# Sparse attention ahead of two expert layers: values' products in runs of four, tails' transposes between the score products, the normaliser's operations one per iteration

## The chip, the core and the metric

One core of a Trainium2 chip runs the whole program. The metric is device time in microseconds (us); lower is better. Five engines work side by side, each in its own program order, and wait for each other by semaphores: TensorE (PE in the rows; its weight loads are PEld), VectorE (DVE), ScalarE (ACT), GpSimd (POOL) and SyncE (SP, which issues most DMAs). Matrix products end in PSUM, which has eight banks of 512 f32 columns on 128 partitions.

## The reference, cut to what matters

```python
def _attn_ref(q, k, v, tau):                     # 4 batches, 8 heads, 576 tokens, 64 columns
    scores = 1.0 / np.sqrt(64) * np.matmul(q, k.transpose(0, 1, 3, 2))
    thresh = np.max(scores, axis=-1, keepdims=True) - tau
    scores = np.where(scores >= thresh, scores, -1000000000.0)
    attn = np.exp(scores - np.max(scores, axis=-1, keepdims=True))
    attn = attn / (np.sum(attn, axis=-1, keepdims=True) + 1e-09)
    return np.matmul(attn, v)
```

The result, as 2304 rows of 512, goes through a layer of eight experts (each row goes to its best one: 512 to 1024, relu, back to 512, times its gate) and then through a dense layer (512 to 2048, x times sigmoid(1.702 x), back to 512).

## The kernel before, in words

**Units and iterations.** Attention works on 16 pairs of heads, four per batch. A pair is cut into nine *units*, w = 0 to 8. Units 0 to 7 are 128 queries (chunk c) of one head (h) each, with w = 2c + h; unit 8 holds the last 64 queries of both heads, and its score product takes eight matmuls instead of four. `run` goes through 144 units, two per *iteration*; 72 iterations make scores, a 73rd only finishes. Nine iterations are a *round*: two pairs. Place k is the iteration's number modulo 9; unit 8 stands first in place 4 and second in place 8.

**An iteration.** In the order in which they are written, which is the order on each engine:

- PE: `qk` of the first unit (score products into two of four PSUM banks `sc`), `trans` of the first unit of the iteration before (four transposes into a bank `tr`), then `qk` and `trans` of the second units, then work that is dealt out by tables: *items* of the values' products (`AV`), `trans_tails`, items of output rows (`ROW`). In the last batch other tables (`AVL`, `ROWL`) count, and items of the router are dealt between.
- DVE: `max` of both units (reads `sc`, line 250), `mask` of both (reads `sc` again, line 280).
- ACT: a copy of the first transposes (`AT`, line 309), `exp` of both units, a copy of the second transposes, then copies of what the dealt work left in PSUM.

`qk` of a unit writes the two banks that `mask` of the unit two before it read, so the first `qk` of an iteration waits for the first `mask` of the iteration before it.

**Values' products.** For each half of a pair's 576 queries (288 columns) `av_items` makes a *tail item* (one product with all 128 columns of `Vt`, line 349) and four *main items* (each one product for each head, 64 columns of the array wide, line 353), all added up in the one bank `av`; after the last, ACT copies it to `xT` (line 358). All ten items of a pair are queued when the pair's last unit has been transposed. On the chip each of these f32 products is two matmuls, so a row of a main item counts four and a tail item two.

**Tails.** Keys 512 to 575 of both heads are transposed by `trans_tails`: after units 3 and 8, behind the iteration's values' products, with one ACT copy of 256 columns each (line 334) and two more copies of 64 by 64 behind unit 8 (line 337).

**Normaliser and rows.** Behind the `mask` of the last unit of every second pair, four small DVE operations (lines 286 to 289) make `r`. A row item (`row_items`) is four matmuls on `xT` (line 383), an ACT copy `xr` (line 388), two POOL products with `r` (lines 391 and 396) and DMAs of `xrow` to `x_dram`; `xr` and `xrow` have two buffers each. When all five row items of the second half of a batch are out, the router of that batch is queued.

**Hand-over.** What is left of the values' and row items behind the 73rd iteration is drained by `tail`, partly between the first transposes (line 947) and products (line 975) of the first expert slot.

```python
            for i in range(2):
                if i < len(us):
                    self.qk(us[i])
                if i < len(ts):
                    copies += self.trans(ts[i])
            ...
            n = AVL[it - IT_LAST] if last else AV[it % 9]
            while n and avq:
                avq.pop(0)()
                n -= 1
            for u in ts:
                self.trans_tails(u)
```

Of the kernel before, what the change touches and what calls it, by code (L numbers as in the profile page):

```python
# [33 lines left out]
CO = (0, 3)  # L34
# [13 lines left out]
ROW = (1, 1, 0, 0, 0, 1, 0, 1, 1)  # L48

class Attention:  # L50
# [16 lines left out]
    def __init__(self, ctx, late_ctx, tc, kq, v, tau, w_gate, x_dram, router, ident, ps):  # L67
# [4 lines left out]
        self.ps_sc, self.ps_tr, self.ps_av = ps  # L72
        P = lambda name, bufs, **kw: ctx.enter_context(tc.tile_pool(name=name, bufs=bufs, **kw))
        Q = lambda name, bufs: late_ctx.enter_context(tc.tile_pool(name=name, bufs=bufs, side="right"))
# [27 lines left out]
        self.extra = []  # L102

# [122 lines left out]
    def qk(self, u):  # L226
        nc = self.nc
        p, w = divmod(u, UPP)
        d = self.st[p]
        sc = self.ps_sc.tile([128, 2, 512], F32, name="sc")  # L230
        d["sc", w] = sc
        if w < 8:
            c, h = divmod(w, 2)
            ops = [(d["qT"][:, h * 768 + c * 128:h * 768 + (c + 1) * 128], kk, h * 704) for kk in ("kA", "kB")]
        else:
            ops = [(d["qT"][:, 512 + h * 128:640 + h * 128], kk, h * 768) for h in range(2) for kk in ("kA", "kB")]
        for hf in range(2):
            for i, (l, kk, c0) in enumerate(ops):
                nc.tensor.matmul(  # L239
                    sc[:, hf, 0:288], l, d[kk][:, c0 + hf * 288:c0 + (hf + 1) * 288],  # L240
                    start=(i == 0), stop=(i == len(ops) - 1),
                )

    def max(self, u):
# [5 lines left out]
        nc.vector.tensor_scalar(  # L250
            e, d["sc", w][:, :, 0:288], self.taue[:, 0:1], 3.0e38, op0=ALU.add, op1=ALU.min, accum_out=thr)
# [6 lines left out]
    def mask(self, u):  # L258
# [17 lines left out]
        else:  # L276
# [3 lines left out]
        nc.vector.scalar_tensor_tensor(  # L280
            out=E.rearrange("p (a c) -> p a c", a=2), in0=d["sc", w][:, :, 0:288],
            scalar=d["thr", w][:, 0:1], in1=d["e", w], op0=ALU.is_le, op1=ALU.mult, accum_out=acc,
        )
        if hp % 2 and w == 8:
            h0 = 2 * hp - 2
            nc.vector.tensor_copy(rs[0:64, 4, h0:h0 + 4:2], rsT[0:64, hp - 1:hp + 1])
            nc.vector.tensor_copy(rs[0:64, 4, h0 + 1:h0 + 4:2], rsT[64:128, hp - 1:hp + 1])
            nc.vector.tensor_scalar_add(r[:, :, h0:h0 + 4], rs[:, :, h0:h0 + 4], 1e-9)
            nc.vector.reciprocal(r[:, :, h0:h0 + 4], r[:, :, h0:h0 + 4])


    def trans(self, u):
# [9 lines left out]
        copies = []  # L302
# [5 lines left out]
        if w < 8:  # L308
            copies.append(lambda: nc.scalar.copy(  # L309
                AT[:, h, :, c * 128:(c + 1) * 128], tp.rearrange("p (k c) -> p k c", k=4)))  # L310
        else:
            copies.append(lambda: nc.scalar.copy(
                AT[:, :, :, 512:576].rearrange("p h k c -> p k h c"),
                tp.rearrange("p (k h c) -> p k h c", k=4, h=2)))
        return copies

    def trans_tails(self, u):
# [3 lines left out]
        if w not in (3, 8):  # L321
            return
        d = self.st[p]
        ATt = d["ATt"]
        c0 = 0 if w == 3 else 2
        t2 = self.ps_tr.tile([128, 512], F32, name="tr")
        for i in range(2):
            nc.tensor.transpose(  # L328
                t2[:, i * 128:(i + 1) * 128],
                d["E", c0 + i].rearrange("p h s -> p (h s)")[:, 512:640], self.ident,  # L330
            )
        if w == 8:
            nc.tensor.transpose(t2[0:64, 256:384], d["E", 4][:, 512:576], self.ident)
        nc.scalar.copy(ATt[:, c0 * 128:(c0 + 2) * 128], t2[:, 0:256])
        if w == 8:
            for i in range(2):
                nc.scalar.copy(ATt[i * 64:(i + 1) * 64, 512:576], t2[0:64, 256 + i * 64:320 + i * 64])


    def av_items(self, p):  # L340
# [3 lines left out]
        xT = self.xT[b, hp] = self.xtp.tile([128, S], F32, name="xT")  # L344
        items = []
        for hf in range(2):
            def tail(hf=hf):
                d["av"] = self.ps_av.tile([128, 512], F32, name="av")
                nc.tensor.matmul(d["av"][:, 0:288], d["Vt"], d["ATt"][:, hf * 288:(hf + 1) * 288], start=True, stop=False, skip_group_check=True)  # L349

            def main(kc, hf=hf):
                for h in range(2):
                    nc.tensor.matmul(  # L353
                        d["av"][h * 64:(h + 1) * 64, 0:288], d["V"][:, h, kc, :],
                        d["AT"][:, h, kc, hf * 288:(hf + 1) * 288], start=False, stop=(kc == 3), skip_group_check=True,
                    )
                if kc == 3:
                    nc.scalar.copy(xT[:, hf * 288:(hf + 1) * 288], d["av"][:, 0:288])
                    if hf == 1:
                        del self.st[p]  # L360

            items.append(tail)
            items += [lambda kc=kc, m=main: m(kc) for kc in range(4)]
        return items
# [44 lines left out]
    def run(self):  # L409
# [12 lines left out]
        while done < NU:  # L422
# [4 lines left out]
            for p in starts:  # L427
# [4 lines left out]
                for n in range(1 if p == 0 else p + 2, min(p + 3, NPAIR)):  # L432
                    self.operands(n)
                    self.poolq += [lambda n=n, i=i: self.split(n, i, NPC) for i in range(NPC)]
            copies = []
            for i in range(2):
                if i < len(us):
                    self.qk(us[i])
                if i < len(ts):
                    copies += self.trans(ts[i])  # L440
# [1124 lines left out]
```

## Time and profile before

| what | value |
|---|---|
| time, median of 3 (lowest to highest) | 936.72 us (936.5 to 938.41) |
| profiled execution: its own time | 940.83 us |
| profiled execution: span of the trace | 939.1 us |
| mean granted clock of TensorE | 0.994 |
| PE, DVE, ACT, POOL busy | 900.9, 515.6, 454.2, 224.7 us |

A busy PE is not a PE at its peak: matmuls overlap in the rows. In a row of the trace in order of time stand the start (us from the span's start), the duration, engine, line, operation, names (output<-inputs), and in brackets the idle time before it and who ended it. Attention takes the first 305 us of the span.

### The profile page before, as it was taken

What the parts mean: (1) busy time and instruction counts of PE and PEld (TensorE: products, weight loads), DVE (VectorE), ACT (ScalarE), POOL (GpSimd) and SP (SyncE); (2) the same over time, 40 slices, a digit from 0 to 9 for tenths busy, and PEclk for the clock granted to TensorE, in tenths of its full rate; (3) what the DMA queues carried; (4) which work ended last, traced back from release to release, by engine and by line L of the source; (5) the groups of instructions that cost most, each with busy time, mean ns of one, the idle gap of its engine ahead of it and who ended that gap; (6) DMA issues with size and microseconds to landing.
All of it is one profiled execution on the core that took longest, in us unless ns stands there. A gap on an engine that the chain in (4) does not pass through costs nothing.

```text
span 939.1 us, 13971 instructions
## 1 busy us (share of the span) xinstructions
PE 900.9 (96%) x5015; PEld 735.8 (78%) x5015; DVE 515.6 (55%) x1129; ACT 454.2 (48%) x820; POOL 224.7 (24%) x299
## 2 busy tenths in 40 slices
PE   8899999999988999999999999999999999999994
PEld 7677777777766578878888988888888888888894
DVE  6788888888889357477777568821211111211110
ACT  6677777777766343445464545522222222222221
POOL 4746565665613220110440000010001000100100
PEclk9999999999999999999999999999999999999998
DMA  7755765656422633656665354410001000100100
GB/s 208 175 139 145 195 177 151 147 127 157 107 49 52 191 124 100 199 172 221 194 214 203 112 149 151 150 45 1 23 23 46 6 12 6 45 0 1 45 1 25
DMA packets 64523, 100.72 MB, mean 107 GB/s; under 512 B 10596, under 2 KB 35970, under 8 KB 64450
## 3 DMA queue, kind: packets, MB, share of 16 engines
q1 hardware_dynamic: 61138, 89.84, 33.1%
q0 software_dynamic: 3312, 9.94, 3.3%
q8 instruction: 42, 0.69, 0.3%
q14 instruction: 31, 0.25, 0.1%
HBM read 63.97 MB, written 17.11 MB: 86 GB/s over the span
## 4 chain that ended last, share of the span: by engine, by line
PE 77%; DVE 8%; issue 6%; DMA 3%; POOL 2%; ACT 2%; SPq 1%; POOLq 0%; ACTq 0%; DVEq 0%
PE tr L975 28%; PE sc L1000 19%; PE sc L1019 9%; PE sc L239 8%; PE av L353 5%; PE tr L307 4%; DVE e L250 3%; DVE E L280 2%; PE tr L383 1%; PE av L349 1%; ACT e L256 1%; PE tr L328 1%; DMA xg<-x_dram,igaA 1%; PE av L947 1%; SPq L176 1%
## 5 line engine op out<-in xcount | busy, mean ns | idle before, releaser
L1212 DVE TENSOR_TENSOR hl<-sg,hh 128x512 fp32r<-128x512 f32 (+1 forms) x80 | 51.0, 638 | 262.2 <-ACT hh L1210 262.2
L1209 ACT ACTIVATE sg<-tr 128x512 f32<-128x512 f32 (+1 forms) x80 | 44.3, 554 | 228.1 <-PE tr L975 228.1
L250 DVE TENSOR_SCALAR_CACHE_REDUCE e<-sc,taue 128x576 f32<-128x576 f32 x144 | 116.6, 813 | 33.5 <-PE sc L239 28.5
L256 ACT ACTIVATE e<-e,thr 128x576 f32<-128x576 f32 x144 | 111.3, 776 | 29.5 <-DVE e L250 28.8
L239 PE MATMUL sc<-kA,qT 128*128 128x288 f32 x320 | 103.0, 338 | 14.9 <-DVE E L280 11.0
L1000 PE MATMUL sc<-wo_h,hh 128*128 128x512 f32 x288 | 112.2, 390 | 0.0
L1000 PE MATMUL sc<-wo_l,hh 128*128 128x512 f32 x288 | 112.2, 390 | 0.0
L1000 PE MATMUL sc<-wo_h,hl 128*128 128x512 f32 x288 | 112.0, 389 | 0.0
L280 DVE SCALAR_TENSOR_TENSOR E<-sc,thr,e 128x576 f32<-128x576 f32 x128 | 103.6, 815 | 8.4 <-ACT e L256 4.4
L309 ACT COPY AT<-tr 128x512 f32<-128x512 f32 x128 | 74.0, 578 | 39.5 <-PE tr L307 39.4
L239 PE MATMUL sc<-kB,qT 128*128 128x288 f32 x320 | 90.0, 297 | 2.0 <-DMA kB<-kB 1.1
L239 PEld LDWEIGHTS sc<-kA,qT 128*128 128x128 f32 x320 | 60.7, 190 | 32.0 <-issue 20.0
L975 PE MATMUL tr<-xl,wi_h 128*128 128x512 f32 (+1 forms) x320 | 78.7, 368 | 0.0
L975 PE MATMUL tr<-xh,wi_l 128*128 128x512 f32 (+1 forms) x320 | 78.7, 368 | 0.0
L975 PE MATMUL tr<-xh,wi_h 128*128 128x512 f32 (+1 forms) x320 | 78.6, 368 | 0.0
L307 PE MATMUL tr<-ident,E 128*128 128x128 f32 x512 | 76.8, 272 | 0.0
L353 PE MATMUL av<-AT,V 128*64 128x288 f32 x512 | 76.7, 419 | 0.0
L975 PEld LDWEIGHTS tr<-xh,wi_h 128*128 128x128 f32 x320 | 57.6, 188 | 11.1
L975 PEld LDWEIGHTS tr<-xh,wi_l 128*128 128x128 f32 x320 | 56.9, 188 | 10.0
L975 PEld LDWEIGHTS tr<-xl,wi_h 128*128 128x128 f32 x320 | 56.9, 189 | 10.0
L239 PEld LDWEIGHTS sc<-kB,qT 128*128 128x128 f32 x320 | 61.0, 191 | 3.0 <-DVE kB L220 1.3
L1000 PEld LDWEIGHTS sc<-wo_h,hl 128*128 128x128 f32 x288 | 54.1, 188 | 11.4
(219 smaller groups left out, 1562.8 us busy)
## 6 DMA issues: line engine op xcount, KB each, us to landing
ra<-in_moe_w_dram SPq DMA_DIRECT2D x20, 512.0 KB, 3.6
rb<-in_moe_w_dram SPq DMA_DIRECT2D x20, 512.0 KB, 3.9
F<-in_kq_dram SPq DMA_DIRECT2D x15, 640.0 KB, 5.1
cv_raw<-in_moe_w_in_dram SPq DMA_DIRECT2D x16, 512.0 KB, 4.8
cv_raw<-in_moe_w_out_dram SPq DMA_DIRECT2D x16, 512.0 KB, 3.7
V<-in_vp_dram SPq DMA_DIRECT2D x16, 320.0 KB, 4.6
kA<-kA SPq DMA_DIRECT2D x15, 320.0 KB, 3.3
kB<-kB SPq DMA_DIRECT2D x15, 320.0 KB, 3.6
```

Of the source, the lines that this page charges most:

```text
L239: nc.tensor.matmul(sc[:, hf, 0:288], l, d[kk][:, c0 + hf * 288:c0 + (hf + 1) * 288], start=(i == 0), stop=(i == len(ops) - 1),)
L250: nc.vector.tensor_scalar(e, d["sc", w][:, :, 0:288], self.taue[:, 0:1], 3.0e38, op0=ALU.add, op1=ALU.min, accum_out=thr)
L256: self.nc.scalar.activation(d["e", w], d["e", w], ACTF.Exp, bias=d["thr", w][:, 0:1], scale=-1.0)
L280: nc.vector.scalar_tensor_tensor(out=E.rearrange("p (a c) -> p a c", a=2), in0=d["sc", w][:, :, 0:288], scalar=d["thr", w][:, 0:1], in1=d[ ...
L307: nc.tensor.transpose(tp[:, kc * 128:(kc + 1) * 128], E[:, k0 + kc * 128:k0 + (kc + 1) * 128], self.ident)
L309: copies.append(lambda: nc.scalar.copy(AT[:, h, :, c * 128:(c + 1) * 128], tp.rearrange("p (k c) -> p k c", k=4)))
L353: nc.tensor.matmul(d["av"][h * 64:(h + 1) * 64, 0:288], d["V"][:, h, kc, :], d["AT"][:, h, kc, hf * 288:(hf + 1) * 288], start=False, stop ...
L975: nc.tensor.matmul(hps[:, 0:T], w[:, kd, :], blk[x][:, kd, 0:T], start=(i == 0), stop=(i == 11))
L1000: nc.tensor.matmul(y, h[:, cs], w, start=(f == 0 and i == 0), stop=(f == blk["nf"] - 1 and i == 2))
L1019: nc.tensor.matmul(blk["y"][d], w[:, ds], h[:, 0:T], start=(f == 0 and i == 0), stop=(f == last and i == 2))
L1209: nc.scalar.activation(sg, hps, ACTF.Gelu_apprx_sigmoid)
L1212: return [upper, lambda: nc.vector.tensor_sub(hl, sg, hh.bitcast(F32))]
```

## The change

- **Values' products.** The tail item goes behind the four main items of its half instead of ahead of them. The tables give four main items to one iteration and the tail item to the next: `AV` is 4, 1, 4, 1, 0, 4, 1, 4, 1 by place. A half's items are queued by `trans_tails`, so the first half of a pair starts before its last units. `AV1`, which put one item between the two score products in place 6, is gone. Rows are queued by the last tail item, and one row item goes out per iteration at places 1, 3, 4, 6 and 8.
- **Tails.** `trans_tails` is called in places 4, 6, 8 and 1, between the first `trans` and the second `qk`; it transposes three chunks behind unit 5, and behind unit 8 the fourth chunk and the last queries, so that one ACT copy does where three did. There are six transposes per pair instead of five. ACT's copy of them stands ahead of both `exp`.
- **Normaliser.** The four DVE operations are put in a list, and one is taken per iteration, ahead of the two `mask`.
- **Score banks.** The four banks are one tile; which unit uses which two is as before. Accesses to different banks are declared independent by hand, and the score products no longer wait for PE's own earlier products.
- **Last batch.** `AVL` and `ROWL` follow the same scheme; the 73rd iteration takes a whole half.

```diff
-AV = (3, 2, 3, 2, 3, 3, 2, 2, 2)
+AV = (4, 1, 4, 1, 0, 4, 1, 4, 1)
+TURNS = ((0, 1), (2, 3))
+TAILS = {4: -3, 6: -4, 8: -2, 1: -3}
...
-AVL = (3, 2, 3, 3, 2, 3, 2, 3, 2, 3, 2, 3, 2, 3, 2, 3, 1, 3, 0, 3, 2, 3)
-ROWL = (0, 3, 2, 2, 2, 1, 2, 2, 2, 2, 2, 0, 2, 3, 2, 2, 1, 2, 2, 2, 2, 2)
-AV1 = (0, 0, 0, 0, 0, 0, 1, 0, 0)
+AVL = (4, 1, 4, 1, 0, 4, 1, 4, 1, 4, 1, 4, 1, 0, 4, 1, 4, 1, 5)
+ROWL = (0, 1, 0, 1, 1, 1, 1, 1, 1, 0, 0, 0, 0, 1, 1, 1, 1, 1, 1)
...
-ROW = (1, 1, 0, 0, 0, 1, 0, 1, 1)
+ROW = (0, 1, 0, 1, 1, 0, 1, 0, 1)
...
+            self.norm += [
+                lambda: nc.vector.tensor_copy(rs[0:64, 4, h0:h0 + 4:2], rsT[0:64, hp - 1:hp + 1]),
+                lambda: nc.vector.tensor_copy(rs[0:64, 4, h0 + 1:h0 + 4:2], rsT[64:128, hp - 1:hp + 1]),
+                lambda: nc.vector.tensor_scalar_add(r[:, :, h0:h0 + 4], rs[:, :, h0:h0 + 4], 1e-9),
+                lambda: nc.vector.reciprocal(r[:, :, h0:h0 + 4], r[:, :, h0:h0 + 4]),
+            ]
...
+        cs = range(3) if w == 5 else range(3, 4)
+        n = len(cs) * 128
         t2 = self.ps_tr.tile([128, 512], F32, name="tr")
+        if w == 8:
+            nc.tensor.transpose(t2[:, 64:192], d["E", 4][:, 448:576], self.ident)
+            nc.tensor.transpose(t2[0:64, 128:256], d["E", 4][:, 512:576], self.ident)
+            n += 64
...
+        self.avq += self.av_items(p, w // 8)
+        return lambda: nc.scalar.copy(ATt[:, cs[0] * 128:cs[0] * 128 + n], t2[:, 0:n])
...
+        def tail():
+            nc.tensor.matmul(d["av"][:, 0:288], d["Vt"], d["ATt"][:, cols], start=False, stop=True, skip_group_check=True)
+            nc.scalar.copy(xT[:, cols], d["av"][:, 0:288])
+            if hf == 1:
+                del self.st[p]
+                if p % 2:
+                    while self.norm:
+                        self.norm.pop(0)()
+                    self.rowq.extend(self.row_items(b, hp // 2))
+
+        return [lambda kc=kc: main(kc) for kc in range(4)] + [tail]
...
+                    copies.append(self.trans(ts[i]))
+                if i == 0 and it > 1 and k in TAILS:
+                    copies.append(self.trans_tails(2 * it + TAILS[k]))
             for i in range(2):
+                while i == 0 and len(copies) > 1:
+                    copies.pop(0)()
                 if i < len(us):
                     self.max(us[i])
                     self.exp(us[i])
...
+            for c in copies:
+                c()
             while rest:
                 rest.pop(0)()
+            if self.norm:
+                self.norm.pop(0)()
...
+        self.trans_tails(NU - 1)()
```

Three places in the program show what moves on PE. The first is the end of iteration 47 and the start of iteration 48 (place 2, then place 3), from the second unit's transposes (`tr<-ident,E`) through the dealt work to the next score products (`sc`). Before:

```order
L307 MATMUL tr<-ident,E 128x128 x3
L353 MATMUL av<-AT,V 64x288 x6
L328 MATMUL tr<-ident,E 128x128 [waits Activation_49]
L328 MATMUL tr<-ident,E 128x128
L239 MATMUL sc<-kA,qT_135 128x288 [waits DVE_49,PE_49]
```

After:

```order
L330 MATMUL tr<-ident,E 128x128 x3
L374 MATMUL av<-AT,V 64x288 [waits Activation_49]
L374 MATMUL av<-AT,V 64x288 x7
L244 MATMUL sc<-kA,qT_136 128x288 [waits DVE_49]
L244 MATMUL sc<-kB,qT_136 128x288
```

Three main items (six products) have become four (eight), the two tails' transposes are gone from here, and the score product waits for DVE alone. The second place is iteration 51 (place 6), from the first unit's transposes to the second unit's score products. Before:

```order
L307 MATMUL tr<-ident,E 128x128 [waits Activation_49]
L307 MATMUL tr<-ident,E 128x128 x3
L349 MATMUL av<-ATt,V 128x288 [waits DMAHW3_49,Activation_49]
L239 MATMUL sc<-kA,qT_136 128x288 [waits DVE_49]
L239 MATMUL sc<-kB,qT_136 128x288
```

After:

```order
L330 MATMUL tr<-ident,E 128x128 [waits Activation_49]
L330 MATMUL tr<-ident,E 128x128 x3
L348 MATMUL tr<-ident,ET 128x128 [waits Activation_49]
L349 MATMUL tr<-ident,ET 64x128
L352 MATMUL tr<-ident,E 128x128
L244 MATMUL sc<-kA,qT_137 128x288 [waits DVE_49]
```

Where one tail item stood ahead of the second score products, three tails' transposes stand now; places 1, 4 and 8, which had nothing there, have them too. The third place is the hand-over, from the last transposes of attention (`ET`) to the first products of the first expert slot (`xh`); `xg` are that slot's gathered rows, `G,xT` is a row item's product. Before:

```order
L353 MATMUL av<-AT,V 64x288 x6
L349 MATMUL av<-ATt,V 128x288
L353 MATMUL av<-AT,V 64x288 x2
L947 MATMUL tr<-ident,xg 128x128 x4
L353 MATMUL av<-AT,V 64x288 x4
L947 MATMUL tr<-ident,xg 128x128 x4
L353 MATMUL av<-AT,V 64x288 x2
L349 MATMUL av<-ATt,V 128x288
L947 MATMUL tr<-ident,xg 128x128 x4
L353 MATMUL av<-AT,V 64x288 x4
L947 MATMUL tr<-ident,xg 128x128 x4
L353 MATMUL av<-AT,V 64x288 x4
```

After:

```order
L374 MATMUL av<-AT,V 64x288 x8
L380 MATMUL av<-ATt,V 128x288
L968 MATMUL tr<-ident,xg 128x128 x4
L414 MATMUL tr<-G,xT 128x144 x4
L968 MATMUL tr<-ident,xg 128x128 x4
L414 MATMUL tr<-G,xT 128x144 x4
L968 MATMUL tr<-ident,xg 128x128 x4
L414 MATMUL tr<-G,xT 64x144 x2
L968 MATMUL tr<-ident,xg 128x128 x4
L996 MATMUL tr<-xh,ah 128x512 x4
```

Before, thirteen values' items stand behind the last transposes, mostly between those of `xg`, and all five row items follow the slot's first group of products; after, ten values' items stand ahead of `xg`, the five row items stand between its transposes, and nothing is left behind the first group.

## Rows read from the trace of the kernel before

**Rows 1.** The page: span and number of instructions.
```profile
span 939.1 us, 13971 instructions
```

**Rows 2.** Groups, us 83 to 226.11; count | busy us, mean ns | idle before, ended by.
```profile
L250 DVE TENSOR_SCALAR_CACHE_REDUCE e<-sc,taue 128x576 f32<-128x576 f32 x72 | 58.1, 813 | 15.3 <-PE sc L239 12.9
L239 PE MATMUL sc<-kA,qT 128*128 128x288 f32 x160 | 51.3, 338 | 4.1 <-DVE E L280 4.1
```

**Rows 3.** DVE in order of time, iterations 45 to 54: the `max` of some units.
```profile
190.19 0.80 DVE L250 TENSOR_SCALAR_CACHE_REDUCE e<-sc,taue 128x576 f32<-128x576 f32 x1
...
197.51 0.82 DVE L250 TENSOR_SCALAR_CACHE_REDUCE e<-sc,taue 128x576 f32<-128x576 f32 x1
198.48 0.82 DVE L250 TENSOR_SCALAR_CACHE_REDUCE e<-sc,taue 128x576 f32<-128x576 f32 x1
201.43 0.82 DVE L250 TENSOR_SCALAR_CACHE_REDUCE e<-sc,taue 128x576 f32<-128x576 f32 x1 [0.40 <-PE sc L239]
...
205.46 0.82 DVE L250 TENSOR_SCALAR_CACHE_REDUCE e<-sc,taue 128x576 f32<-128x576 f32 x1 [0.52 <-PE sc L239]
...
209.58 0.81 DVE L250 TENSOR_SCALAR_CACHE_REDUCE e<-sc,taue 128x576 f32<-128x576 f32 x1
...
213.02 0.82 DVE L250 TENSOR_SCALAR_CACHE_REDUCE e<-sc,taue 128x576 f32<-128x576 f32 x1
214.47 0.82 DVE L250 TENSOR_SCALAR_CACHE_REDUCE e<-sc,taue 128x576 f32<-128x576 f32 x1 [0.62 <-PE sc L239]
217.04 0.81 DVE L250 TENSOR_SCALAR_CACHE_REDUCE e<-sc,taue 128x576 f32<-128x576 f32 x1
...
220.90 0.82 DVE L250 TENSOR_SCALAR_CACHE_REDUCE e<-sc,taue 128x576 f32<-128x576 f32 x1 [0.28 <-PE sc L239]
...
224.99 0.16 DVE L286 COPY rs<-rsT 64x2 f32<-64x2 f32 x1
...
226.11 0.81 DVE L250 TENSOR_SCALAR_CACHE_REDUCE e<-sc,taue 128x576 f32<-128x576 f32 x1
```

**Rows 4.** PE in order of time, iterations 47 and 48.
```profile
196.67 0.40 PE L239 MATMUL sc<-kA,qT 128*128 128x288 f32 x1
...
198.80 1.68 PE L353 MATMUL av<-AT,V 128*64 128x288 f32 x12
200.41 0.44 PE L328 MATMUL tr<-ident,E 128*128 128x128 f32 x2
...
202.62 0.65 PE L349 MATMUL av<-ATt,V 128*128 128x288 f32 x2
203.21 0.71 PE L353 MATMUL av<-AT,V 128*64 128x288 f32 x4
```

**Rows 5.** DVE's end of a `mask` and PE's next score product, iterations 48 and 49.
```profile
203.90 0.08 DVE L280 DVE_READ_ACCUMULATOR E<-sc,thr,e 128x1 f32 x1
...
204.13 0.37 PE L239 MATMUL sc<-kA,qT 128*128 128x288 f32 x1 [0.22 <-DVE E L280]
```

**Rows 6.** Hand-over in order of time, PE and two rows of ACT.
```profile
306.48 0.60 PE L307 MATMUL tr<-ident,ET 128*128 128x128 f32 x4
306.92 0.38 PE L328 MATMUL tr<-ident,E 128*128 128x128 f32 x2
...
318.74 1.21 PE L975 MATMUL tr<-xh,ah 128*128 128x512 f32 x4
...
321.63 1.14 PE L383 MATMUL tr<-G,xT 128*128 128x144 f32 x8
...
323.26 0.70 ACT L388 COPY xr<-tr 128x288 f32<-128x288 f32 x2
...
325.78 1.19 PE L975 MATMUL tr<-xh,ah 128*128 128x512 f32 x4 [0.67 <-ACT xr L388]
...
331.99 0.39 ACT L388 COPY xr<-tr 64x288 f32<-64x288 f32 x1 [5.50 <-POOL lgt L396]
...
333.38 1.20 PE L1019 MATMUL sc<-hh,bh 128*128 128x512 f32 x4 [1.87 <-ACT bh L1244]
```

More of the change, by code (lines that the diff above doesn't have):

```diff
@@ L102, in __init__ @@
         self.extra = []
+        self.norm = []
+        self.writes, self.reads = {}, {}
     def gate_setup(self):
@@ L229, in qk, with read, ring, apart @@
         d = self.st[p]
-        sc = self.ps_sc.tile([128, 2, 512], F32, name="sc")
-        d["sc", w] = sc
+        order = self.ring(u)
+        lo, hi = sorted(order)
+        d["sc", w] = self.banks[:, lo:lo + 2, 0:288]
+        c, h = divmod(w, 2)
         if w < 8:
-            c, h = divmod(w, 2)
             ops = [(d["qT"][:, h * 768 + c * 128:h * 768 + (c + 1) * 128], kk, h * 704) for kk in ("kA", "kB")]
         else:
-            ops = [(d["qT"][:, 512 + h * 128:640 + h * 128], kk, h * 768) for h in range(2) for kk in ("kA", "kB")]
-        for hf in range(2):
+            ops = [(d["qT"][:, 512 + i * 128:640 + i * 128], kk, i * 768) for i in range(2) for kk in ("kA", "kB")]
+        for bank in order:
+            k0 = 288 * int(bank == hi)
             for i, (l, kk, c0) in enumerate(ops):
-                nc.tensor.matmul(
-                    sc[:, hf, 0:288], l, d[kk][:, c0 + hf * 288:c0 + (hf + 1) * 288],
+                m = nc.tensor.matmul(
+                    self.banks[:, bank, 0:288], l, d[kk][:, c0 + k0:c0 + k0 + 288],
                     start=(i == 0), stop=(i == len(ops) - 1),
-                )
+                ).ins
+                self.apart(m, u, (bank,), self.reads)
+                self.writes.setdefault(u, []).append((m, (bank,)))
+    def read(self, u, ins):
+        self.apart(ins.ins, u, self.ring(u), self.writes)
+        self.reads.setdefault(u, []).append((ins.ins, self.ring(u)))
+    def ring(self, u):
+        return TURNS[u % 2]
+    def apart(self, ins, u, banks, others):
+        for v in range(u - 8, u + 2):
+            for o, b in others.get(v, ()):
+                if not set(b) & set(banks):
+                    self.tc.declare_no_dep(ins, o, reason="these banks are read and written by turns of their own")
     def max(self, u):
@@ L343, in av_items, with main, values @@
         d = self.st[p]
[L344 to L347, printed above, removed]
-                d["av"] = self.ps_av.tile([128, 512], F32, name="av")
[L349 to L364, printed above, removed]
+        if hf == 0:
+            self.xT[b, hp] = self.xtp.tile([128, S], F32, name="xT")
+        xT = self.xT[b, hp]
+        cols = slice(hf * 288, (hf + 1) * 288)
+        def main(kc):
+            if kc == 0:
+                d["av"] = self.ps_av.tile([128, 512], F32, name="av")
+            for h in range(2):
+                nc.tensor.matmul(
+                    d["av"][h * 64:(h + 1) * 64, 0:288], d["V"][:, h, kc, :],
+                    d["AT"][:, h, kc, cols], start=(kc == 0), stop=False, skip_group_check=True,
+                )
+        def tail():
[8 more added lines that the diff above has]
+        return [lambda kc=kc: main(kc) for kc in range(4)] + [tail]
+    def values(self, n):
+        while n and self.avq:
+            n -= 1
+            self.avq.pop(0)()
     def row_items(self, b, hh):
```

88 lines of the change are left out of this document (26 added, 62 removed).

## The prediction

> **What bounds the kernel now.** The kernel is two stages, and only the first is changed: attention up to about 305 us, then expert layers in which TensorE works nearly without a pause. A gain in attention is therefore a gain in the time at which the expert slots begin, and that is all that can be won. The profiled execution took 940.83 us, of which 939.1 are the trace [rows 1] and 1.7 lie around it; it is 4.1 us above the median of 936.72. The sum below is a difference, worked out inside this one execution, and is then set on the median.
>
> I read the stretch from 83 us to 226.11 us first, because it is four whole rounds: (226.11 - 83.0) / 4 = 35.78 us a round, 3.98 an iteration. The groups of that stretch show two engines that wait for each other: `max` stood 12.9 us behind PE's score products, and these stood 4.1 us behind `mask` [rows 2]. So no engine is full; an iteration is a loop, `qk` to `max` to `mask` to the next `qk`, and whichever half is longer sets its length.
>
> Next DVE in order of time, with iterations measured from one first `max` to the next [rows 3]. The reader is to see three kinds. The floor is place 5: 209.58 to 213.02, 3.44 us, with no wait. Where PE has more to do, `max` waits: place 2, 197.51 to 201.43, 3.92 us. And place 8, 220.90 to 226.11, is 5.21 us, of which 1.12 (224.99 to 226.11) are the normaliser's four operations with nothing beside them. The round from 190.19 to 226.11 is 35.92.
>
> Last PE in place 2 [rows 4]. From the first `qk` at 196.67 to the first values' product at 198.80 are 2.13 us for both units' products and transposes. Three main items then take 198.80 to 200.41, 1.61 us. Twelve products as one entry are busy 1.68 us and four are busy 0.71, so an item is (1.68 - 0.71) / 2 = 0.485 us, and entering and leaving the run costs about 0.71 - 0.485 = 0.23. A tail item takes 202.62 to 203.21, 0.59. A transpose is 0.11: four between 306.48 and 306.92 [rows 6].
>
> **Values' products in runs of four.** An iteration with four mains has on PE 2.13 + 4 x 0.485 + 0.23 = 4.30 us, or, from the measured run of three, 2.13 + 1.61 + 0.485 = 4.23. I take 4.23. That is above the floor of 3.44, so in places 0, 2, 5 and 7 `max` will wait for PE, and whatever DVE does there is hidden. Four such iterations are 16.92 us. What the runs save is the number of entries: eight runs of mains a round become four, 4 x 0.23 = 0.9 us of PE. It is worth something only in iterations that PE sets. The lower bound of such an iteration is 2.13 + 4 x 0.485 = 4.07, if the entry were hidden behind the transposes.
>
> Here a rule bears on the entries. The Trainium skill, "TensorEngine Tiling (Array Packing)", Key Properties, says that a change of tiling mode drains the engine; the main items use 64 columns of the array and everything around them 128, so each run is two such changes. This trace agrees with about 0.23 us per run. By the rule alone fewer runs must be faster, and that is rival B.
>
> **Tails' transposes between the score products.** They leave the end of the iteration, where they were PE's work ahead of the next `qk`, and go ahead of the second `qk` in places 1, 4, 6 and 8. The nearest row is place 6 of before, where a tail item stood in that very gap: the distance from first to second `max` was 213.02 to 214.47, 1.45 us, against 197.51 to 198.48, 0.97, elsewhere [rows 3], and the iteration, 213.02 to 217.04, took 4.02, 0.58 over the floor. Three transposes are 0.33 us instead of 0.59, so I take 0.33 for the iteration. Below, it could be nothing, if the second `qk` had that much slack (place 6 says that it has hardly any); above, 0.58, because ACT's copy of the tails now stands ahead of both `exp` and may delay the first. So places 4 and 6 become 3.44 + 0.33 = 3.77 each.
>
> **The normaliser, one operation per iteration.** 1.12 us leave place 8: 5.21 - 1.12 = 4.09, and with the transposes 4.42. The operations reappear in places 0 to 3, 0.28 us each. In 0 and 2 they lie inside DVE's wait for PE; if that cover were gone they would cost 0.28 each. In 1 and 3 they stand ahead of `mask` on DVE, and the next `qk` waits for that. Place 1 becomes 3.44 + 0.33 + 0.28 = 4.05. Place 3 took 201.43 to 205.46, 4.03 us, because the product of the next unit has eight matmuls; it becomes 4.31.
>
> **Score banks.** From the end of a `mask` (203.90 + 0.08 = 203.98) to the `qk` that waits for it (204.13) are 0.15 us [rows 5]. The order shows that this product now waits for DVE alone. Five places end in such a wait; if half of 0.15 goes in most of them that is 0.25 to 0.4 a round, with bounds of 0 and 0.75. I take 0.3. The banks themselves go in the same turn as before and change nothing else.
>
> **Sum of a round.** 16.92 + 4.05 + 4.31 + 3.77 + 3.77 + 4.42 - 0.3 = 36.94, against 35.78. Some of the terms overlap (an iteration after one that PE set begins with DVE in arrears of nothing, and a late second `max` can hide in a place that waits anyway), so I take two thirds of the difference of 1.16, which is 0.8 us a round. The bounds are 4 x 4.07 + 3.72 + 4.03 + 3.44 + 3.44 + 4.09 - 0.75 = 34.25, that is -1.5, and 36.94 + 0.3 + 4 x 0.25 for delayed `exp` = 38.2, that is +2.5. Six rounds give **+4.8 us** (-9 to +15). The odd iterations at the start I take as unchanged.
>
> **Last batch and hand-over.** Behind attention's last transposes 10 items are left instead of 13; the three others, 3 x 0.485 = 1.5 us, are done in iterations that PE sets already: **+1.4 us** there. Before, from 306.92 to the first slot's first group at 318.74 PE did values' items and the transposes of `xg`; the group took 2.89 us, to 321.63; then the five rows 4.15 us, with PE waiting 0.67 of it for ACT's `xr`, until the second group at 325.78 [rows 6]. After, PE's work in the same stretch is ten items (8 x 0.485 + 2 x 0.59 + two runs' 0.23 + a wait of 0.5 for `xT` = 6.0), sixteen transposes of `xg` with their entries (2.3), rows without waits (2.5) and the group (2.9): 13.7 us, so that the second group could begin at about 321, 4.8 us earlier. Also the 1.87 us at 333.38, where PE waited for `bh` behind ACT's last `xr`, could go: 6.7 us at best. Against it: the row buffers are two, and the chain from the first `xr` copy at 323.26 to the last at 331.99 took 8.7 us, 5.50 of them ACT waiting for POOL. Now the casts of `xh`, which the first group needs, are queued behind the same copies on ACT. With the first copy at about 313.5, the same chain ends at 322.2, a cast later the first group starts at 323, and the second at 326: nothing gained but part of the 1.87. Between -6.7 and +0.3 I take **-3.5**, the middle.
>
> Together +4.8 + 1.4 - 3.5 = **+2.7 us**: 939.4 from the median (943.5 for an execution like the profiled one). Differences below 0.2%, 1.9 us, are about what a measurement of this kernel can't tell from no change.
>
> **The rivals.**
>
> A, the forecast: a run of four makes an iteration that PE sets, and the round is 0.4 to 2 us longer; slower by 2 to 9 us, 939 to 946. For it: 4.23 against 3.44. Chance 0.46.
>
> B, faster: PE's total sets the round, not its distribution. Before, 12.9 us in four rounds were waits for PE [rows 2], 3.2 a round, and 1.12 the exposed normaliser. If the score products, the transposes and the four mains overlap better than the one run of three shows, the four iterations cost 4.07 and less, the normaliser is hidden whole and the tails' transposes cost nothing: 34.25 to 35.5 a round, up to -9 us, and with the hand-over -3 to -13: 924 to 934. The point from which it decides is the iteration with four mains: at 3.95 and below the round is shorter than before. Against it: place 2 has 2.13 us of work ahead of the mains, and nothing of it is removed. Chance 0.29.
>
> C, no change: attention loses 3 to 6 us and the hand-over gives them back, or both are about nothing; within 1.9 us of 936.72. Speaks for it that PE has the same products in total and that the stretch of loss and the one of gain are about equally large. Chance 0.25, in which I count the cases where the wait at the banks and the entries pay for the unequal iterations.
>
> **How the numbers follow.** A is the likeliest, and its middle, with the hand-over as taken, is 939.4; its own range is 938 to 946. The range of 8 in 10 reaches through C into the milder half of B, to 930.5, and ends at 945.5: faster 0.29, same 0.25, slower 0.46.
>
> **What would show it.** In the changed kernel's rows of DVE, places 0, 2, 5 and 7 should be 4.1 to 4.3 us long with `max` waiting for PE at their ends; the distance from first to second `max` in places 1, 4 and 6 should be about 1.3; no stretch of four small operations should stand between `mask` and `max`; the wait from `mask` to `qk` should be under 0.1. A round should be 36.2 to 37. In the hand-over the second group should start 1 to 5 us sooner after the last transposes, with ACT's last `xr` copy ahead of the last `xh`. The prediction is wrong if the places with four mains are below 4.0, if places with one item fall to 3.44 despite the transposes, or if the first group waits for ACT behind the rows by more than 5 us.

## The result and the profile after

The changed kernel takes 943.96 us (median of 4, 942.9 to 946.41) against 936.61 us before (936.72 in the runs shown ahead): a ratio of 1.008, 95% interval 1.0063 to 1.0097. It is slower, by 7.35 us where +2.7 was forecast; the time lies in the range given.

The page of the kernel after, and the groups that answer to [rows 2], from 82.63 to 231.95 us, again four rounds:

```profile
span 941.1 us, 13870 instructions
```
```profile
L272 DVE TENSOR_SCALAR_CACHE_REDUCE e<-sc,taue 128x576 f32<-128x576 f32 x72 | 58.5, 817 | 21.7 <-PE sc L244 20.1
L244 PE MATMUL sc<-kA,qT 128*128 128x288 f32 x160 | 51.2, 337 | 9.7 <-DVE E L302 5.3 <-DVE ET L302 3.2 <-issue 1.2
```

Four rounds take 149.3 us instead of 143.1. Both waits have grown: `max` stands 20.1 us behind PE (12.9 before), and PE's score products stand 8.5 us behind `mask` (4.1 before). Neither engine has much more work: in this stretch PE is busy 139.6 us (139.0 before) and DVE 123.6 (121.9). They wait for each other more.

DVE after, iterations 45 to 54, as in [rows 3], with one operation of the router:

```profile
194.38 0.81 DVE L272 TENSOR_SCALAR_CACHE_REDUCE e<-sc,taue 128x576 f32<-128x576 f32 x1
...
198.50 0.82 DVE L272 TENSOR_SCALAR_CACHE_REDUCE e<-sc,taue 128x576 f32<-128x576 f32 x1 [0.24 <-PE sc L244]
199.79 0.82 DVE L272 TENSOR_SCALAR_CACHE_REDUCE e<-sc,taue 128x576 f32<-128x576 f32 x1 [0.46 <-PE sc L244]
...
202.56 0.82 DVE L272 TENSOR_SCALAR_CACHE_REDUCE e<-sc,taue 128x576 f32<-128x576 f32 x1
...
206.79 0.82 DVE L272 TENSOR_SCALAR_CACHE_REDUCE e<-sc,taue 128x576 f32<-128x576 f32 x1 [0.70 <-PE sc L244]
...
210.84 0.82 DVE L272 TENSOR_SCALAR_CACHE_REDUCE e<-sc,taue 128x576 f32<-128x576 f32 x1 [0.51 <-PE sc L244]
212.13 0.82 DVE L272 TENSOR_SCALAR_CACHE_REDUCE e<-sc,taue 128x576 f32<-128x576 f32 x1 [0.47 <-PE sc L244]
...
215.29 0.80 DVE L272 TENSOR_SCALAR_CACHE_REDUCE e<-sc,taue 128x576 f32<-128x576 f32 x1
...
218.49 1.48 DVE L672 TENSOR_TENSOR L<-L,bias 128x40 f32<-128x40 f32 x1
219.88 0.81 DVE L272 TENSOR_SCALAR_CACHE_REDUCE e<-sc,taue 128x576 f32<-128x576 f32 x1
...
223.32 0.82 DVE L272 TENSOR_SCALAR_CACHE_REDUCE e<-sc,taue 128x576 f32<-128x576 f32 x1
...
227.54 0.82 DVE L272 TENSOR_SCALAR_CACHE_REDUCE e<-sc,taue 128x576 f32<-128x576 f32 x1 [0.59 <-PE sc L244]
...
231.95 0.81 DVE L272 TENSOR_SCALAR_CACHE_REDUCE e<-sc,taue 128x576 f32<-128x576 f32 x1
```

Place 2, with four mains, is 202.56 to 206.79, 4.23 us, and `max` waits 0.70 us at its end. Places 1 and 4 have the second `max` 1.29 us behind the first (198.50 to 199.79, 210.84 to 212.13) where it was 0.97. The round is 37.57 us against 35.92.

PE after, place 2 (to [rows 4]); and, place 4, the end of a `mask` on DVE with the `qk` behind it (to [rows 5]):

```profile
201.72 0.40 PE L244 MATMUL sc<-kA,qT 128*128 128x288 f32 x1 [0.41 <-DVE E L302]
...
203.86 2.16 PE L374 MATMUL av<-AT,V 128*64 128x288 f32 x16
205.95 0.40 PE L244 MATMUL sc<-kA,qT 128*128 128x288 f32 x1
```
```profile
213.69 0.09 DVE L302 DVE_READ_ACCUMULATOR ET<-sc,thr,e 128x1 f32 x1
```
```profile
213.83 0.40 PE L244 MATMUL sc<-kA,qT 128*128 128x288 f32 x1 [0.81 <-DVE ET L302]
```

From `qk` to `qk` are 4.23 us (201.72 to 205.95) with no wait inside. In place 4 PE stands 0.81 us: `mask` was late, since `max` was late, since the second score product was late. From `mask` to `qk` are now 0.05 us.

The hand-over after, PE with one row of ACT (to [rows 6]):

```profile
320.45 1.15 PE L414 MATMUL tr<-G,xT 128*128 128x144 f32 x8
...
327.17 1.19 PE L996 MATMUL tr<-xh,ah 128*128 128x512 f32 x4 [1.91 <-ACT xr L419]
...
330.02 1.07 PE L996 MATMUL tr<-xh,ah 128*128 128x512 f32 x4
...
335.46 0.84 PE L1040 MATMUL sc<-hh,bh 128*128 128x512 f32 x3
```
```profile
326.73 0.39 ACT L419 COPY xr<-tr 64x288 f32<-64x288 f32 x1 [1.48 <-POOL lgt L427]
```

The first group waits for ACT behind the last `xr`, 1.91 us; from the first group to the first product with `bh` are 8.3 us instead of 14.6 (12.6 in a second profile of the kernel before, before_again below).

### The profile page after: what moved, and what is told of

It is laid out like the page before. It is cut to its first block, busy times and chain, and to the rows that moved or that the text cites. A ratio compares the mean times of both kernels' runs of the same rounds, so it can differ in the third digit from the quotient of the medians.

```text
span 941.1 us, 13870 instructions
## 1 busy us (share of the span) xinstructions
PE 897.7 (95%) x5031; PEld 742.9 (79%) x5031; DVE 516.2 (55%) x1129; ACT 448.5 (48%) x788; POOL 223.0 (24%) x299
## 4 chain that ended last, share of the span: by engine, by line
PE 77%; DVE 9%; issue 7%; DMA 3%; ACT 2%; POOL 1%; SPq 1%; POOLq 0%; ACTq 0%
PE tr L996 28%; PE sc L1021 19%; PE sc L244 9%; PE sc L1040 8%; PE av L374 6%; PE tr L330 4%; DVE e L272 3%; DVE E L302 3%; DMA cv_raw<-in_moe_w_in_dram 1%; PE tr L352 1%; DVE bl L1266 1%; SPq L179 1%; DVE ET L302 1%; ACT e L278 1%; PE av L968 1%
## 5 line engine op out<-in xcount | busy, mean ns | idle before, releaser
L374 PE MATMUL av<-AT,V 128*64 128x288 f32 x512 | 70.1, 416 | 0.2 <-ACT xT L381 0.2
L330 PEld LDWEIGHTS tr<-ident,E 128*128 128x128 f32 x512 | 63.0, 141 | 0.4 <-issue 0.4
L1021 PEld LDWEIGHTS sc<-wo_h,hl 128*128 128x128 f32 x288 | 54.0, 188 | 11.3
```

The source lines that it names most:

```text
L330: nc.tensor.transpose(tp[:, kc * 128:(kc + 1) * 128], E[:, k0 + kc * 128:k0 + (kc + 1) * 128], self.ident)
L374: nc.tensor.matmul(d["av"][h * 64:(h + 1) * 64, 0:288], d["V"][:, h, kc, :], d["AT"][:, h, kc, cols], start=(kc == 0), stop=False, skip_gr ...
L1021: nc.tensor.matmul(y, h[:, cs], w, start=(f == 0 and i == 0), stop=(f == blk["nf"] - 1 and i == 2))
```

## The experiments

Times, and three stretches of each trace: six rounds (first `max` of iteration 9 to that of 63), the end of the last batch (63 to 71, below called the last batch), and the hand-over (first `max` of 71 to the first product with `bh`), in us. The last batch begins at iteration 54, so the sixth of the six rounds already follows `AVL`. The times are medians; the stretches are those of one profiled execution each. The ratio is to the kernel before on the same chip.

| kernel | time | ratio, 95% | 9 to 63 | 63 to 71 | 71 to bh |
|---|---|---|---|---|---|
| before, profile shown ahead | 936.72 | | 216.41 | 36.37 | 32.72 |
| before_again | 936.38 | | 216.45 | 36.40 | 31.20 |
| after | 943.96 | 1.0063 to 1.0097 | 224.22 | 39.03 | 26.55 |
| tails_behind | 932.62 | 0.9948 to 0.9973 | 214.76 | 38.58 | 26.45 |
| tails_between_before | 945.0 | 1.0077 to 1.0105 | 223.15 | 36.77 | 30.61 |
| even_runs | 948.42 | 1.0104 to 1.014 | 230.98 | 39.01 | 26.54 |
| even_runs_2 | 936.2 | 0.9991 to 1.0016 | 219.69 | 37.59 | 26.55 |
| tails_behind_even | 933.91 | 0.995 to 0.9982 | 215.88 | 38.55 | 26.55 |
| norm_block | 945.95 | 1.0088 to 1.012 | 225.43 | 37.02 | 26.56 |
| norm_dealt_alone | 937.08 | 0.9992 to 1.0014 | 216.06 | 37.51 | 32.85 |
| banks_alone | 936.61 | 0.9995 to 1.0015 | 215.71 | 36.30 | 30.28 |
| last_filled | 931.55 | 0.9919 to 0.9956 | 214.81 | 36.29 | 26.89 |
| late_items | 932.37 | 0.9932 to 0.9969 | 214.73 | 39.82 | 26.56 |
| rows_behind | 933.3 | 0.9957 to 0.9977 | 214.64 | 39.79 | 27.13 |

**before_again**, no edit.

> The kernel before, unchanged, for a second profile. Its first profiled execution took 940.83 us, 4.1 above the median of its other runs, and the two profiles put the hand-over's gain at 6.2 us (the first expert group starts 8.4 us later in the changed kernel, the second product of the slot only 2.0 us later), while the medians differ by 7.35 us. Theory 1: the first profile caught the kernel before with an unusually long wait for the row buffers; then this one is 2 to 4 us shorter, nearly all of it between the first group and the first product on bh, and the hand-over of the change gives back only 2 to 4 us. Theory 2: the hand-over always gives back 6 us, and the first profile's 4 us lie elsewhere, spread over the span; then the hand-over reads the same again. Iteration lengths in attention should be the same by both, 35.6 and 36.0 us for even and odd rounds.

Both theories were half right. The rounds read the same, and the time from `bh` to the end is 605.7 and 605.6 us. The first profile was 3.0 us late at iteration 9 (47.88 against 44.84) and 1.5 us longer in the hand-over, where the 1.87 us wait for `bh` is missing now. Against this second profile, the change's 6.6 us of span are: +0.8 up to iteration 9, +7.8 in six rounds, +2.6 in the last batch, -4.65 in the hand-over. Two of these carry the accidents of single profiles: the fourteen traces reach iteration 9 at anything from 43.6 to 47.9 us, and the five traces with the old order of the hand-over read 30.28 to 32.85 us for it, so the change gains 3.7 to 6.3 us there.

**tails_behind**

```diff
-                if i == 0 and it > 1 and k in TAILS:
-                    copies.append(self.trans_tails(2 * it + TAILS[k]))
...
             self.values(n)
+            if it > 1 and k in TAILS:
+                self.trans_tails(2 * it + TAILS[k])()
```

> The changed kernel with the tails' transposes moved back behind the values' products (places 4, 6, 8 and 1 as in the change, but no longer ahead of the second score product). Theory 1, by the sum of the prediction: each of the four places loses the 0.32 us by which the second max is late, so places 4 and 6 fall to 3.45, place 8 to 4.0 and place 1 to 3.7; a round gets 1.3 us shorter, 35.6 instead of 36.9, and the time falls by 9 to 11 us to 933 to 935, under the kernel before. Theory 2: TensorE's total work sets the round; the same transposes then cost as much at the end of the iteration, and the time stays within 2 us of 944.

Theory 1. In the round of iterations 18 to 26, places 4 and 6 are 3.45 us each (3.82 and 3.76 in the changed kernel), place 1 is 3.74 (4.06), place 8 is 3.96 (4.30); the places with four mains stay at 4.23. The 11.3 us taken back are more than the change lost; 9.5 of them lie in the six rounds.

**tails_between_before**, the same move made in the kernel before:

```diff
                 if i < len(ts):
                     copies += self.trans(ts[i])
+                if i == 0:
+                    for u in ts:
+                        self.trans_tails(u)
...
-            for u in ts:
-                self.trans_tails(u)
```

> The kernel before with its tails' transposes moved between the first unit's transposes and the second unit's score product, ACT's copies of them ahead of both exp; all else as before. They stand in places 2, 5, 7 and 0: two transposes in 2 and 7, three in 5 and 0. Theory 1 (the move costs only where TensorE has nothing to do at the iteration's end, since there the second score product, and so max and mask, are what the next iteration waits for; where values' items fill the iteration to its end, the transposes are only taken from behind them): places 2, 7 and 0 are within 0.1 us of 3.92, 3.9 and 3.6, and place 5 grows from 3.44 to between 3.75 and 4.0; a round is 0.3 to 0.7 us longer and the time 2 to 5 us, 938.5 to 941.5. Theory 2 (each such group costs its transposes and more, wherever it stands): each of the four places grows by 0.22 to 0.5 us, a round by 1.1 to 1.7, and the time is 944 to 949.

Where it costs is as by theory 1: iterations 45 to 53 have place 2 at 4.00 (3.91 before), 7 at 3.90 (3.86), 0 at 3.62 (3.58), and only the thin place 5 grows, from 3.44 to 4.13 (to 4.48 to 4.50 in four of the six rounds). The price there was set too low: three copies stand ahead of `exp` on ACT, and in place 5 DVE's first `mask` waits for that `exp` too:

```profile
216.84 0.82 DVE L280 SCALAR_TENSOR_TENSOR E<-sc,thr,e 128x576 f32<-128x576 f32 x1 [0.65 <-ACT e L256]
```

The six rounds lose 6.7 us; the time, 945.0, is above what theory 1 allowed and in the range of theory 2, whose places it does not fit.

**even_runs** (the first line added) and **even_runs_2** (the second)

```diff
-AV = (4, 1, 4, 1, 0, 4, 1, 4, 1)
+AV = (3, 2, 3, 2, 1, 3, 2, 2, 2)
+AV = (3, 2, 3, 2, 1, 3, 1, 3, 2)
```

> The changed kernel with the values' items dealt as 3, 2, 3, 2, 1, 3, 2, 2, 2 over the places, in the first three batches alone; all else is as changed. Eight runs of mains a round instead of four. Theory 1 (an iteration with four mains is over-full, and those with one item leave TensorE idle): places 0, 2 and 5 fall from 4.23 to 3.75, place 7 to 3.5, while places 1, 3 and 8, which get a main item more, grow by 0.2 to 0.3; a round is 0.8 to 1.2 us shorter and the time 5 to 7 us, 937 to 939. Theory 2 (fewer runs are what counts, each entry costs 0.23 us): four entries more make a round 0.9 us longer, 949.

The time spoke for theory 2, but one row of PE shows another cause:

```profile
110.31 0.71 PE L374 MATMUL av<-AT,V 128*64 128x288 f32 x4 [1.64 <-ACT xT L381]
```

A main item behind a tail item begins a new sum in the one bank `av`, which ACT first has to empty; place 6 took 5.79 us, while places 0, 2 and 5 fell to 3.75 as expected.

> The changed kernel with the values' items dealt as 3, 2, 3, 2, 1, 3, 1, 3, 2 in the first three batches, so that, unlike in even_runs, no main item follows a tail item in the same iteration: there place 6 took 5.8 us because the main item waited 1.64 us for ACT's copy out of the one bank av. Theory 1: that wait was what made even_runs slow, and evenly dealt items are better than runs of four; places 0, 2, 5 and 7 are 3.75, place 6 is 3.76, places 1, 3 and 8 4.4, 4.3 and 4.6, a round 35.9, and the time 936 to 938. Theory 2: the number of runs decides; a round is longer than 37 and the time over 944.

Theory 1, number by number: 3.75, 4.42, 3.75, 4.29, 3.84, 3.75, 3.76, 3.76, 4.59, a round of 35.9 (37.0 where the router works on DVE), and the time of the kernel before. The transposes stand where the change put them, and the deal alone takes 4.5 us off the six rounds.

**tails_behind_even**: the kernel of tails_behind with `AV = (3, 2, 3, 2, 0, 3, 2, 3, 2)`.

> The kernel of tails_behind with the values' items of the first three batches dealt 3, 2, 3, 2, 0, 3, 2, 3, 2 instead of 4, 1, 4, 1, 0, 4, 1, 4, 1 (no main item behind a tail item). Theory 1 (the changed kernel lost because an iteration was over-full and its neighbour idle): here too the uneven deal costs, and a round gets 0.5 to 1.5 us shorter, the time 925 to 929. Theory 2 (with the tails' transposes behind the values, TensorE is busy in the places with one item too, so nothing is left to even out, and four more runs cost 0.23 us each): a round gets 0.5 to 0.9 us longer, the time 935 to 938.

Theory 2, milder than either range: the six rounds are 1.1 us longer. Only the first five are dealt anew; the first of them is 0.46 us shorter, the other four are 0.26 to 0.56 longer. In iterations 18 to 26 places 0, 2, 5 and 7 win 0.5 us each, and places 1, 3, 6 and 8 lose 0.69, 0.25, 0.63 and 0.65. The intervals of the two times overlap. So an uneven deal costs only where something else keeps the thin iterations long.

**norm_block** and **norm_dealt_alone**. The first puts the four operations of the changed kernel back in one block behind `mask`; the second deals them out in the kernel before:

```diff
+            if self.norm:
+                self.norm.pop(0)()
             for i, u in enumerate(us):
                 self.mask(u)
```

> The changed kernel with the normaliser's four operations again in one block behind the mask of the last unit. Theory 1, by the sum of the prediction: place 8 grows by 0.85 to 1.1 us and places 1 and 3 lose 0.28 each, so a round is 0.3 to 0.6 us longer and the time 2 to 4 us, 946 to 948. Theory 2: dealing them out gained nothing, since the four operations cost as much where they stand now: within 1 us of 944.

> The kernel before with the normaliser's part of the change alone: its four operations one per iteration in places 0 to 3, ahead of the masks. Theory 1, by the terms of the prediction: place 8 loses 1.1 us (5.2 to 4.1), places 0 and 2 hide theirs in VectorE's wait, place 3 gains up to 0.28; a round is 0.7 to 1.0 us shorter and the time 5 to 7 us, 929 to 931. Theory 2: what place 8 loses comes back in the places that follow, because TensorE sets them; under 2 us, 934 to 936.

The first is unclear: 945.95 against 943.96, with intervals that overlap. Place 8 grows to 5.55, but place 0 behind it falls from 4.23 to 3.35 in three rounds; in the next two it stays at 4.44 and 4.24, and the six rounds are 1.2 us longer. The second is theory 2, and no time at all is won. Place 8 falls from 5.16 to 4.27, and place 0 grows from 3.63 to 4.52; at its end DVE waits for PE:

```profile
119.05 0.82 DVE L251 TENSOR_SCALAR_CACHE_REDUCE e<-sc,taue 128x576 f32<-128x576 f32 x1 [0.99 <-PE sc L240]
```

PE has 4.5 us of work in place 0 (three mains, the transposes of three tails, a row). In before_again, with the block still on DVE, PE takes the same 4.51 us from `qk` to `qk` there, with no wait inside:

```profile
113.81 0.39 PE L239 MATMUL sc<-kA,qT 128*128 128x288 f32 x1
...
118.32 0.40 PE L239 MATMUL sc<-kA,qT 128*128 128x288 f32 x1
```

While DVE did its block, PE was already at it. In the kernel before, the block looked exposed on DVE, and dealing it out gained nothing.

**banks_alone**: `qk`, `max` and `mask` on the one tile of four banks, in the kernel before.

> The kernel before with the part on score banks alone: one tile of four banks, with the accesses to different banks declared independent, so that a score product no longer waits for TensorE's own earlier products. Theory 1, by the prediction's term: the wait from the end of a mask to the product that stands behind it falls from 0.15 to 0.05 us, a round gets 0.3 us shorter, the time 2 us, 934. Theory 2: where the product waits for VectorE, the loop has slack elsewhere, and the time stays within 1 us of 936.2.

Theory 2 by time. The round of iterations 45 to 53 is 0.1 us shorter (35.81), place 3 by 0.07; the term was three times too large.

**late_items** (`AVL` ends in 2 instead of 5) and **rows_behind**:

```diff
-        att.tail(2)
+        att.values(2)
```

> The kernel of tails_behind with two values' items instead of five in the 73rd iteration, so that thirteen are left for the hand-over and all five row items again stand behind the first slot's first group of products, as in the kernel before. Theory 1: the place of the rows is what the hand-over gains by; the first group starts within 0.6 us of where it did, the second 4 us later, and the time rises by 4 to 5 us to 936 to 938. Theory 2: the same work is only moved past the first group; within 1.5 us of 932.6.

> The kernel of tails_behind with the five row items again behind the first slot's first group of products (between the transposes of xg only values' items are taken). late_items was meant to do this and didn't: its rows still went out ahead of that group, and it tells only that thirteen items left are as good as ten. Theory 1: the rows' place is what the hand-over gains by, since PE there waits for ACT's copies of the rows twice and then runs the next group late; the first group starts 1 to 3 us sooner, the second 1 to 3 us later, and the time rises by 1.5 to 4 us to 934 to 937. Theory 2: TensorE's work up to the second group is the same either way; within 1 us of 932.6.

late_items did not put the rows behind the first group and tells only that thirteen items left instead of ten make no difference that can be seen. rows_behind did: its first group starts 13.7 us after iteration 71 instead of 18.2, the first product with `bh` 0.7 us later than in tails_behind. That is theory 2: the rows' place is worth 0.7 us in that stretch and by time (933.3 against 932.62, inside the intervals), which these runs can't tell from nothing. The 39.8 us that both kernels read for the last batch are not their edits' doing: iteration 70 takes 7.25 us at a granted clock of 0.67, against 6.0 at 0.85 in tails_behind.

**last_filled**

```diff
-AVL = (4, 1, 4, 1, 0, 4, 1, 4, 1, 4, 1, 4, 1, 0, 4, 1, 4, 1, 5)
+AVL = (4, 1, 4, 1, 0, 4, 1, 4, 1, 4, 1, 2, 3, 0, 2, 3, 4, 1, 5)
```

> The kernel of tails_behind with the values' items of the last batch dealt otherwise from iteration 64 on: 1, 2, 3, 0, 2, 3, 4, 1, 5 instead of 1, 4, 1, 0, 4, 1, 4, 1, 5. In tails_behind iteration 69, in which VectorE is filled by the router for 5.5 us, has one tail item and a row item on TensorE; TensorE then stands 2.9 us, and behind it the granted clock reads 0.54 for 3.5 us. Theory 1: the thin iteration is the cause; with three items in it TensorE waits under 1.5 us, the clock stays at 1.00, iterations 64 to 71 get 2 to 3 us shorter, and the time falls to 930 or 931. Theory 2: the router's work on VectorE sets these iterations, and the clock would be lost in any case; within 1 us of 932.6.

In this one trace it is theory 1. Two stretches of windows of tails_behind, then of last_filled (us, PE, PEld, DVE, ACT and POOL busy, granted clock, DMA share, GB/s):

```profile
287.00:290.20 3.20, 0.34 (x3) 0.12 (x1) 3.20 (x9) 2.28 (x5) 0.00 (x0) 0.97 0.07 17
290.20:293.70 3.50, 3.47 (x16) 3.44 (x17) 2.06 (x7) 1.81 (x5) 1.06 (x3) 0.54 0.17 27
```
```profile
287.00:290.50 3.50, 2.05 (x14) 1.67 (x13) 3.47 (x11) 2.61 (x6) 0.15 (x1) 1.00 0.02 4
290.50:293.50 3.00, 3.00 (x38) 2.65 (x38) 2.81 (x9) 2.06 (x5) 0.92 (x3) 1.00 0.19 30
```

With items in iteration 69 PE waits 1.45 us at its end instead of 2.89, and the clock stays; the last batch is 36.29 us instead of 38.58. Of these 2.3 us 1.4 lie in iterations 69 and 70, which the clock had stretched, and 0.7 in iteration 65, which has two items less. The time falls by 1.1 us, within the intervals. It is the fastest kernel of this study, 0.6% under the kernel before.

That the thin iteration causes the loss of the clock is not shown, though. norm_block and even_runs_2 have the changed kernel's tables here and the same wait, and their profiles keep the clock. First the changed kernel, then norm_block: the wait, and the window of iteration 70 (columns as above):

```profile
301.52 0.40 PE L244 MATMUL sc<-kA,qT 128*128 128x288 f32 x1 [2.88 <-DVE E L302]
302.39:308.92 6.53, 6.53 (x53) 4.86 (x52) 3.60 (x15) 2.94 (x5) 2.76 (x4) 0.74 0.23 48
```
```profile
303.28 0.40 PE L244 MATMUL sc<-kA,qT 128*128 128x288 f32 x1 [2.87 <-DVE E L302]
304.15:309.23 5.08, 5.08 (x53) 4.00 (x52) 3.57 (x15) 2.94 (x5) 1.91 (x4) 1.00 0.18 33
```

The same matrix products take 6.53 us at a clock of 0.74 and 5.08 at 1.00 (5.07 in even_runs_2, behind a wait of 2.90). So the loss falls on some executions of a kernel and not on others: of even_runs_2's ten, five had a mean clock of 0.996 and took 935.26 to 936.06 us, the other five 0.993 or 0.994 and 936.33 to 938.49. last_filled's six read 0.993 to 0.996 and tails_behind's six 0.991 to 0.994, which speaks for the fuller iteration without settling it; and medians that differ by 1 or 2 us, as norm_block's from the changed kernel's and last_filled's from tails_behind's, may differ by this alone.

## Why the prediction came out as it did

**The direction was right, and not for the reason given.** A's reason was the run of four, 4.23 us against the floor of 3.44. tails_behind has the same 4.23 in the same places and is 0.4% faster than the kernel before. What makes the change slower is the place of the tails' transposes, a term of the sum that A does not name. Of the three parts of the sum, +4.8, +1.4 and -3.5 were said for rounds, last batch and hand-over, and +7.8, +2.6 and -4.65 measured.

**Right: four mains are 4.23 us.** Of the twelve such iterations in three rounds (18 to 35 and 45 to 53) ten read 4.12 to 4.24; two, with the router's work beside them, 4.6. The length of each place came out almost as summed, in the round of iterations 18 to 26: place 1 4.06 (4.05 said), place 3 4.06 (4.31), place 4 3.82 and place 6 3.76 (3.77), place 8 4.30 (4.42), and the round 36.93 against the sum of 36.94. That last agreement is partly luck: places 3 and 8 came out 0.37 shorter than said, and stand in for the -0.3 of the banks.

**Wrong: "I take two thirds of the difference".** The discount for overlapping terms had no row behind it. With the sum as it stood, six rounds would have been +7.0; they measured +7.8. These are not six times the same: the first five grew by 1.35 to 1.83 us each, and the sixth, in the last batch, got 0.2 shorter. The sum also left out the router. It describes a round without the router's operations on DVE, but was set against 35.78, the mean of four rounds of which some have them: iterations 18 to 26 were 35.58 before, so that such a round grew by 1.35. In place 4 the sum starts from the floor of 3.44, where the round of [rows 3] took 4.12 (205.46 to 209.58). After the change two of the rounds (from 27 and from 45) have a router operation in place 5 that takes 1.48 us, against 0.20 before and in tails_behind; place 5 is 4.6 us there, and these rounds are 37.7 and 37.6. Why it takes 1.48 is not shown.

**Wrong in its reading: the normaliser.** "1.12 us leave place 8" is nearly true (0.89 in norm_dealt_alone) and worth nothing in the kernel before: PE's work of place 0 stands behind it. The term did no harm to the sum, because places 0 and 8 were both summed anew.

**Right in size, overlooked in weight: the tails.** They were listed as one term among several, 0.33 us in each of four places; against tails_behind they are 0.31 to 0.37 there in iterations 18 to 26, and in two rounds 1.0 more in place 5. This term decides the sign: without it the six rounds are 1.7 us shorter than before instead of 7.8 longer, and the time, 932.62, lies in the range of rival B. Not by B's mechanism, though: the iterations with four mains stay at 4.23, and B wanted 4.07 and less. Nor is it the only way back: even_runs_2 leaves the transposes and, by an even deal, reaches the time of the kernel before. The rule behind B (the Trainium skill, "TensorEngine Tiling (Array Packing)", Key Properties) is borne out weakly: four runs more a round cost 1.1 us over five rounds in tails_behind_even, 0.06 us a run. The prediction had 0.23 us of PE's time per run, from durations; by the starts of the rows four mains take 2.09 us (203.86 to 205.95), 0.15 more than four times 0.485.

**The last batch.** +1.4 was said, +2.6 measured. 1.4 of the 2.6 are the clock, which the sum did not have: even_runs_2, with the same tables there and its clock kept, reads 37.59, 1.2 over before_again, and norm_block 37.02. That 1.2 is close to +1.4 does not show that it is the three items; no run moves them alone.

**Near in size, wrong in cause: the hand-over.** -3.5 was said, the middle of two bounds, and -4.65 measured against before_again (-3.7 to -6.3 by the profile taken). That it came near is luck: it was put down to the five rows and ACT's `xr`, and rows_behind gives them 0.7. Rows of PE in before_again show what else went:

```profile
301.70 0.75 PE L349 MATMUL av<-ATt,V 128*128 128x288 f32 x2 [1.49 <-ACT xT L358]
...
306.55 0.75 PE L349 MATMUL av<-ATt,V 128*128 128x288 f32 x2 [0.50 <-ACT xT L358]
...
312.37 0.75 PE L349 MATMUL av<-ATt,V 128*128 128x288 f32 x2 [0.50 <-ACT xT L358]
```

Three waits for the one bank `av`, 2.5 us, where the changed kernel has one of 0.16. With the rows' 0.7 that is 3.0; the remaining 1.6 us were not separated. That the gain is these waits is read from the rows; no run takes them away alone.

**Banks:** -0.3 a round was said, about -0.1 seen.

## What to carry to other kernels

In a loop of two engines, work on one of them is free at the end of an iteration that the other sets, and costs its full length (and that of the copies that it puts on a third engine) ahead of the product that the loop waits for, unless that engine is busy to the iteration's end anyway, as in places 2, 7 and 0 of tails_between_before; look at where in the iteration a step stands before counting how long it is. A block that stands exposed on one engine may be covering another engine's backlog: read the next iteration too before booking it as a gain. And terms that come from rows are not to be discounted by feeling.

## What the hardware showed that was not expected

PE stood 2.89 us in iteration 69 of tails_behind, and in the window of 3.5 us from the end of that wait the granted clock was 0.54, nearly all at the lower level of 1.2 GHz; the score products then began 0.24 us apart instead of 0.13. The changed kernel had the same, 0.75 and 0.70 in two stretches of 3.1 us behind a wait of 2.88. But the wait does not decide it. Eight profiles have a wait of 2.86 to 2.90 us at this place: six lost the clock around its end, and two, norm_block and even_runs_2, kept it at 1.00. tails_between_before lost it behind a wait of 1.83 (0.67 over iteration 70), and last_filled kept it behind 1.45. The Trainium skill, "TensorE: Matmul & The Clock Gate", HAM oscillation, warns of idle gaps that throttle the engine; here a gap inside one iteration could be enough, and the same gap was not always. In the changed kernel it cost 1.45 us of iteration 70 (6.53, against 5.08 in norm_block), and one profile of a kernel does not tell how often it happens.
